# First x blocks in fp32 on two hardware queues with a cast on ScalarE, and the second group's transposes inside the first K bundle

## Chip, cores, metric

One core of one Trainium2 chip. The metric is the device time of one execution in microseconds (us), as the median of several runs. "Start" below is the first 30 us of the span, up to about the first V matmul; from some 36 us on the matmul engine (PE) has work without a break. SyncE is SP in the profile, ScalarE is ACT, VectorE is DVE, GpSimd is POOL.

## The reference, cut to what matters

```python
# x: (8, 4160, 192), weight: (8 heads, 7 taps)
w = exp(weight - max); w = w / (sum(w) + 1e-9)          # one row of 7 taps for each head
y[b, s, h, :] = sum_k w[h, k] * x[b, s + k - 6, h, :]   # causal convolution, 24 channels a head
y_prev = y shifted by one position
xk = mu_k * y + (1 - mu_k) * y_prev
xr = mu_r * y + (1 - mu_r) * y_prev
k = max(xk @ w_k, 0)                                    # 192 -> 1024
v = (k * k) @ w_v                                       # 1024 -> 192
out = sigmoid(xr @ w_r) * v
```

## The kernel before

x comes in blocks of 120 positions. A block is convolved on PE by a banded matrix for each head (`toe`, built from the softmax of the small `weight` row), copied out of PSUM, transposed on PE, evacuated, mixed with its predecessor (`diff`, `mix`), and multiplied by `w_k`. Blocks come in groups: the first four (3, 4, 4 and 5 blocks of a pair of batches) make up the start. PSUM is the memory that PE writes to, and an evacuation is a copy out of it. `xk` has 192 channels: K's upper half uses the first 128 of them, its lower half the other 64. A step is a stretch of positions that is mixed at once, and a K slot is the part of its K output that fills one PSUM buffer and is read by one relu. The start's loads and its order are the prologue:

```python
def prologue():
    nc.sync.dma_start(out=w_raw, in_=...)      # weight row, to all partitions
    nc.scalar.preload_act_table(AF.Exp)
    nc.vector.memset(ones_t, 1.0)
    x_tile(0, nc.vector)
    nc.vector.memset(zeros, 0.0)
    nc.gpsimd.affine_select(out=ident, ...)
    load_x(0)                                  # GpSimd; the DMA casts fp32 to bf16
    masks_band()
    warm(WARM)                                 # 16 matmuls that only keep PE's clock up
    ...
    softmax()                                  # Exp, then a tiny sigmoid that loads the other table
    make_toe()
    load_x(1); load_wk(); load_x(2); load_wr(); load_wv()     # all GpSimd, in this order
    ...                                        # mu_k, mu_r on SyncE
    for c in range(0, len(chunks(0)), 2):
        conv_mm(0, c)                          # 8 matmuls
    conv_out_first()                           # 5 copies, ScalarE and VectorE in turn
    warm(4)
    tr(0, 0)                                   # transposes, evacuations, diff, mix
    warm(2)
    ...conv(1, c)                              # second group
    warm(3)
    x_tile(3, nc.vector)
    load_x(3)

# main loop, one bundle of four K slots at a time
for part in (ns[:2], ns[2:]) if b == 0 else (ns,):
    k_section(part)                            # K matmuls: upper half, then lower half
    for n in part: k_relu(n)                   # ScalarE
    if part[:1] == ns[:1]: run(first, b)       # transposes of the next group, after K
```

`ring` is a pool of four PSUM buffers of two banks each; every convolution, transpose, K, V and R output takes its next buffer.

## Time and profile before

| | kernel before |
|---|---|
| time, median | 448.14 us (447.26 to 448.17, 3 runs; with a fourth of 447.44, taken beside the kernel after, 447.79) |
| profiled span | 445.9 us |
| PE busy | 433.8 us, 97% |
| first relu of K starts | 14.78 us |
| first V matmul starts | 29.95 us |
| last output is issued | 441.93 us |

How to read it: PE is full from about 36 us on, so the start decides. Two places in it serve as marks. The first relu shows how fast the chain "weight row, toe, convolution, copies, transposes, mix, K" is. The first V matmul shows when the hand-over to the dense part happens; a kernel whose first V matmul is earlier by some time issues its last output earlier by nearly the same: from the one to the other it takes 411.97 to 412.18 us in all 14 traces of this study.

Further lines of the order of time of the kernel before; the columns are start, duration, engine, line, operation, shapes, count, and in brackets the engine's idle time before and what ended it:

```profile
4.23 0.21 DVE L173 TENSOR_REDUCE w_max<-w_raw 128x8 f32<-128x56 f32 x1 [1.89 <-DMA w_raw<-in_weight_dram]
8.63 0.34 ACT L268 CAST y<-ps_c 120x216 bf16<-120x216 f32 x1 [2.14 <-PE ps_c L250]
19.01 2.98 PE L416 MATMUL ps_k<-xk,wk 128*128 128x512 bf16 x16 [1.13 <-DVE xk L397]
29.95 2.80 PE L505 MATMUL ps_v<-wv,k 128*128 128x192 bf16 x32 [0.60 <-ACT k_sb L457]
441.93 0.49 SPq L559 DMA_DIRECT2D out_dram<-o_tail  x1
```

The first copy out of PSUM is at 8.63; PE waits 1.13 us for the second step's xk before 19.01.

### The profile page before, as it was taken

What the parts mean: (1) busy time and instruction counts of PE and PEld (TensorE: products, weight loads), DVE (VectorE), ACT (ScalarE), POOL (GpSimd) and SP (SyncE); (2) the same over time, 40 slices, a digit from 0 to 9 for tenths busy, and PEclk for the clock granted to TensorE, in tenths of its full rate; (3) what the DMA queues carried; (4) which work ended last, traced back from release to release, by engine and by line L of the source; (5) the groups of instructions that cost most, each with busy time, mean ns of one, the idle gap of its engine ahead of it and who ended that gap; (6) DMA issues with size and microseconds to landing.
All of it is one profiled execution on the core that took longest, in us unless ns stands there. A gap on an engine that the chain in (4) does not pass through costs nothing.

```text
span 445.9 us, 9765 instructions
## 1 busy us (share of the span) xinstructions
PE 433.8 (97%) x3937; PEld 304.5 (68%) x3937; DVE 387.8 (87%) x702; ACT 353.7 (79%) x465; POOL 48.2 (11%) x70
## 2 busy tenths in 40 slices
PE   7889999999999999999999999999999999999995
PEld 3555766776866776676676677667667677766685
DVE  4899799889988989889978998889988898999972
ACT  3878888888897788888888788888988778777771
POOL 8650001102020100012020000010200000000000
PEclk9999999999999999999999999999999999999999
DMA  8998759979497693295798493485964562522113
GB/s 89 150 186 157 187 146 160 162 188 197 122 206 194 128 197 103 80 202 138 154 209 167 121 216 114 111 118 160 197 160 115 162 153 80 111 72 71 64 47 114
DMA packets 133184, 63.64 MB, mean 143 GB/s; under 512 B 84723, under 2 KB 132883, under 8 KB 133139
## 3 DMA queue, kind: packets, MB, share of 16 engines
q1 hardware_dynamic: 94834, 48.28, 41.1%
q0 software_dynamic: 38224, 14.68, 29.1%
q8 instruction: 31, 0.51, 0.5%
q14 instruction: 15, 0.11, 0.1%
q10 hardware_dynamic: 80, 0.05, 0.0%
HBM read 29.39 MB, written 36.99 MB: 149 GB/s over the span
## 4 chain that ended last, share of the span: by engine, by line
PE 87%; DVE 3%; DMA 3%; ACT 3%; POOL 2%; issue 1%; DVEq 0%
PE ps_k L416 37%; PE ps_v L505 37%; PE ps_r L500 4%; PE ps_r L501 4%; PE ps_c L250 4%; DMA xb<-in_x_dram 1%; DMA wk<-in_moe_w_k_dram 1%; ACT y L286 1%; DVE k L476 1%; POOL xb L122 1%; ACT r_sb L522 1%; DVE o_sb L532 1%; PE ps_vt L505 0%; DVE xk L397 0%; ACT k_sb L457 0%
## 5 line engine op out<-in xcount | busy, mean ns | idle before, releaser
L457 ACT ACTIVATE k_sb<-ps_k 128x1024 bf16<-128x1024 f32 x260 | 245.9, 1035 | 13.0 <-PE ps_k L416 9.8
L416 PE MATMUL ps_k<-xk,wk 64*128 64x512 bf16 (+3 forms) x1056 | 191.6, 373 | 2.5 <-DVE xk L397 1.7
L505 PEld LDWEIGHTS <-k 128*128 128x128 bf16 x2048 | 170.9, 98 | 14.9 <-issue 0.7
L505 PE MATMUL ps_v<-wv,k 128*128 128x192 bf16 x2048 | 179.4, 246 | 0.6 <-ACT k_sb L457 0.6
L476 DVE TENSOR_TENSOR k<-k_sb 128x1024 bf16<-128x1024 bf16 x256 | 168.2, 686 | 10.2 <-ACT k_sb L457 9.1
L416 PEld LDWEIGHTS <-wk 64*128 64x128 bf16 (+1 forms) x1056 | 66.4, 96 | 102.0 <-issue 56.0
L532 DVE TENSOR_TENSOR o_sb<-ps_v,r_sb 128x768 f32<-128x768 f32 x64 | 61.2, 957 | 26.6 <-PE ps_v L505 26.2
L522 ACT ACTIVATE r_sb<-ps_r 128x768 bf16<-128x768 f32 x64 | 53.1, 829 | 24.8 <-PE ps_r L501 24.8
L286 ACT CAST y<-ps_c 120x480 bf16<-120x480 f32 (+6 forms) x84 | 38.4, 515 | 32.8 <-PE ps_c L250 32.8
L122 POOL DMA_DIRECT2D xb<-in_x_dram x36 | 32.2, 898 | 168.9 <-PE ps_k L416 95.2
L500 PE MATMUL ps_r<-wr,xr 128*128 128x192 bf16 x256 | 47.4, 246 | 0.2 <-DVE o_sb L532 0.2
L501 PE MATMUL ps_r<-wr,xr 128*128 128x192 bf16 x256 | 47.4, 246 | 0.0
L397 DVE TENSOR_TENSOR xk<-xk,yT 128x1024 bf16<-128x1024 bf16 (+1 forms) x66 | 36.2, 549 | 2.3
L397 DVE TENSOR_TENSOR xr<-xr,yT 128x1024 bf16<-128x1024 bf16 (+1 forms) x66 | 36.2, 549 | 2.3
L250 PE MATMUL ps_c<-xb,toe 128*128 128x480 bf16 (+4 forms) x144 | 30.9, 321 | 1.9 <-DMA xb<-in_x_dram 1.9
L355 DVE TENSOR_TENSOR d<-yT 128x1536 bf16<-128x1536 bf16 (+4 forms) x38 | 31.8, 837 | 0.1
L394 DVE TENSOR_SCALAR xk<-d,mu 128x1024 bf16<-128x1024 bf16 (+1 forms) x66 | 27.5, 416 | 1.2
L501 PEld LDWEIGHTS <-xr 128*128 128x128 bf16 x256 | 25.0, 98 | 3.9 <-issue 0.5
L500 PEld LDWEIGHTS <-xr 128*128 128x128 bf16 x256 | 25.0, 98 | 3.5
L394 DVE TENSOR_SCALAR xr<-d,mu 128x1024 bf16<-128x1024 bf16 (+1 forms) x66 | 27.2, 412 | 0.0
L289 ACT CAST y<-ps_c 120x480 bf16<-120x480 f32 (+6 forms) x45 | 20.3, 501 | 8.0 <-PE ps_c L250 8.0
L250 PEld LDWEIGHTS <-toe 128*128 128x128 bf16 x144 | 12.8, 98 | 3.6 <-issue 1.3
(57 smaller groups left out, 79.3 us busy)
## 6 DMA issues: line engine op xcount, KB each, us to landing
out_dram<-o_sb SPq DMA_DIRECT2D x62, 384.0 KB, 3.1
y_dram<-y SPq DMA_DIRECT2D x10, 900.0 KB, 7.0
xb<-in_x_dram POOLq DMA_DIRECT2D x14, 480.0 KB, 8.7
xb<-in_x_dram POOLq DMA_DIRECT2D x6, 432.0 KB, 7.8
xb<-in_x_dram POOLq DMA_DIRECT2D x10, 192.0 KB, 6.4
y_dram<-y SPq DMA_DIRECT2D x3, 450.0 KB, 4.1
y_dram<-y SPq DMA_DIRECT2D x1, 810.0 KB, 5.7
xb<-in_x_dram POOLq DMA_DIRECT2D x2, 384.0 KB, 7.1
```

The lines of the kernel that those rows point to most:

```text
L250: nc.tensor.matmul(out=ps[:, :, :, i * G : (i + 1) * G], lhsT=toe[:, h, :], rhs=xbs[g][:, :nb, :, h * G : (h + 1) * G], start=True, stop=True,
L286: copy(out=yh[:, :, :, c0 : c0 + n], in_=ps[:BLK, :, :, 0:n])
L394: nc.vector.tensor_scalar(out=o, in0=d[:, sl, :L], scalar1=mu[:, i, part : part + 1], scalar2=None, op0=ALU.mult)
L397: nc.vector.tensor_tensor(out=o, in0=o, in1=yT[:, sl, c0 : c0 + L], op=ALU.add)
L416: nc.tensor.matmul(out=ps[:, i, f * L : (f + 1) * L], lhsT=wk[r, 0 if hi else 1, fs], rhs=xk[r, i if hi else 2, :L], start=start and f == ...
L457: nc.scalar.activation(out=k_sb, in_=ps.rearrange("p a b -> p (a b)"), func=AF.Relu)
L476: nc.vector.tensor_tensor(out=o, in0=i, in1=i, op=ALU.mult)
L500: nc.tensor.matmul(out=o, lhsT=hi, rhs=wr[:, 0, :], start=True, stop=False)
L501: nc.tensor.matmul(out=o, lhsT=lo, rhs=wlo, start=False, stop=True)
L505: nc.tensor.matmul(out=o, lhsT=k2s[s][:, f, t * P : (t + 1) * P], rhs=wv[:, f, :], start=(f == 0), stop=(f == NF - 1),)
L522: nc.scalar.activation(out=r_sbs[s, j], in_=ps, func=AF.Sigmoid)
L532: nc.vector.tensor_tensor(out=o_sb.rearrange("p (b t) d -> p b (t d)", b=2), in0=v_ps.pop((s, j)), in1=r_sbs.pop((s, j)), op=ALU.mult,)
```

## The change

Its intent: x for the first group no longer goes through GpSimd's queue, behind masks and three other issues, but comes in fp32 on the queues of SyncE and ScalarE at once, and ScalarE casts it. GpSimd starts on the second group's x and on `w_k` earlier. The small groups' convolution gets a bank layout with three copies in place of five. The second group's transposes move ahead of the first bundle's lower half of K, so that DVE has the second step's xk earlier. The diff's core:

```diff
+    def load_x_first(s, eng):
+        nb = groups[0][2]
+        for q0, q1, n0, n1 in ((0, P, 1, nb), (16, P, 0, 1), (HALO, 16, 0, 1)):
+            eng.dma_start(out=x_f32[q0:q1, n0:n1, s, :], in_=...)
...
         nc.scalar.activation(out=w_exp, in_=w_exp, func=AF.Exp)
+        xbs[0] = three.tile([P, GB, 2, D], BF16, tag="xb", name="xb")
+        for s in range(2):
+            nc.scalar.copy(out=xbs[0][:, : groups[0][2], s, :], in_=x_f32[:, :, s, :])
         nc.scalar.activation(out=w_sig, in_=w_exp[:, 0, 0:1], func=AF.Sigmoid)
...
+    def conv_small(g, copies):            # groups 0 to 2
+        tiles = [ring.tile([P, 2, BANK], FP32, tag="k", name="ps_c") for _ in range(2)]
+        banks = [t[:, i, 0 : nb * P] for t, i in ((tiles[0], 0), (tiles[1], 0), (tiles[0], 1))]
+        ...                               # 15 matmuls, bank by bank
+        for i, o in enumerate(banks):
+            copies[i](out=ys[g][i]..., in_=o[:BLK, :])
...
+        if ns[0] == 0:                    # k_section of the first half bundle
+            k_ps[0] = ring.tile([P, 2, BANK], FP32, tag="k", name="ps_k")
+            warm(k_ps[0], 3)
+            for n in ns:
+                k_mm(n, True, True)
+            run(first, 0)                 # the second group's transposes
+            for n in ns:
+                k_mm(n, False, False)
+            return
...
         nc.sync.dma_start(out=w_raw, in_=...)
+        nc.vector.memset(ones_t, 1.0)
+        nc.vector.memset(x_f32[0:32, 0, :, :], 0.0)
+        load_x_first(0, nc.sync)
+        load_x_first(1, nc.scalar)
         nc.scalar.preload_act_table(AF.Exp)
...
+        load_x(1, (0,))
         nc.gpsimd.affine_select(out=ident, ...)
-        load_x(0)
+        load_x(1, (1,))
+        load_wk(0, NF // 2)
         masks_band()
...
-        load_x(1)
-        load_wk()
+        load_wk(NF // 2, NF)
         load_x(2)
...
-        ...conv_mm(0, c); conv_out_first(); warm(4); tr(0, 0); warm(2); ...conv(1, c); warm(3)
+        conv(0, 0)
+        tr_first()
+        conv(1, 0)
```

Cut: `tr_first` (one evacuation on DVE, one on ScalarE), the fused mix of the first step, and renamings.

More of the change, by code (lines that the diff above doesn't have):

```diff
@@ L106, in x_tile, with load_x @@
             eng.memset(xb[:, nb - 1, :, :], 0.0)
-    def load_x(g):
+    def load_x(g, batches=(0, 1)):
         p, blk0, nb, _, _ = groups[g]
         xb = xbs[g]
-        for s in range(2):
+        for s in batches:
             b = 2 * p + s
@@ L129, in load_x @@
             )
+    def load_x_first(s, eng):
+        nb = groups[0][2]
+        for q0, q1, n0, n1 in ((0, P, 1, nb), (16, P, 0, 1), (HALO, 16, 0, 1)):
+            eng.dma_start(
+                out=x_f32[q0:q1, n0:n1, s, :],
+                in_=bass.AP(
+                    tensor=x.tensor,
+                    offset=x.offset + (s * S + n0 * BLK - HALO + q0) * D,
+                    ap=[[D, q1 - q0], [BLK * D, n1 - n0], [1, D]],
+                ),
+            )
+    x_f32 = three.tile([P, NF * STEP], FP32, tag="k2", name="x_f32")[:, 0 : groups[0][2] * 2 * D].rearrange(
+        "p (n s d) -> p n s d", s=2, d=D
+    )
     w_raw = const.tile([P, H, K], FP32)
@@ L155, with load_wk @@
     tails = [const.tile([P, 2, 2, P], BF16, tag=f"tail{i}", name=f"tail{i}") for i in range(2)]
-    def load_wk():
-        nc.gpsimd.dma_start(out=wk[:, 0, :], in_=moe_w_k[0:P, :])
-        nc.gpsimd.dma_start(out=wk[0:LO, 1, :], in_=moe_w_k[P:D, :])
-        nc.gpsimd.dma_start(out=wk[LO:P, 1, :], in_=moe_w_k[P:D, :])
+    def load_wk(f0, f1):
+        fs = slice(f0 * P, f1 * P)
+        nc.gpsimd.dma_start(out=wk[:, 0, fs], in_=moe_w_k[0:P, fs])
+        nc.gpsimd.dma_start(out=wk[0:LO, 1, fs], in_=moe_w_k[P:D, fs])
+        nc.gpsimd.dma_start(out=wk[LO:P, 1, fs], in_=moe_w_k[P:D, fs])
     def load_wr():
@@ L241, in conv_mm @@
         nb = groups[g][2]
-        if c == 0 and g > 0:
+        if c == 0:
             ys[g] = two.tile([P, GB, 2 * D], BF16, tag="y", name="y")
@@ L256, in conv_mm @@
                 )
-    def conv_out_first():
-        nb = groups[0][2]
-        ys[0] = [const.tile([P, nb, P], BF16, tag=f"y0{i}", name="y0") for i in range(3)]
-        for c, hs in enumerate(chunks(0)):
-            ps = conv_ps.pop((0, c))
-            c0, c1 = hs[0] * G, hs[-1] * G + G
-            n = min(c1, P) - c0
-            if n > 0:
-                for i, copy in enumerate((nc.scalar.copy, nc.vector.tensor_copy)):
-                    copy(out=ys[0][i][:BLK, :, c0 : c0 + n], in_=ps[:BLK, :, i, 0:n])
-            if c1 > P:
-                n = c1 - max(c0, P)
-                lo = ys[0][2][:BLK, :, :].rearrange("p n (s c) -> p n s c", s=2)
-                nc.scalar.copy(out=lo[:, :, :, c1 - P - n : c1 - P], in_=ps[:BLK, :, :, c1 - c0 - n : c1 - c0])
+    def conv_small(g, copies):
+        nb = groups[g][2]
+        ys[g] = [two.tile([P, 4, P], BF16, tag=f"y_small{i}", name="y_small") for i in range(3)]
+        tiles = [ring.tile([P, 2, BANK], FP32, tag="k", name="ps_c") for _ in range(2)]
+        banks = [t[:, i, 0 : nb * P] for t, i in ((tiles[0], 0), (tiles[1], 0), (tiles[0], 1))]
+        for i, o in enumerate(banks):
+            o = o.rearrange("p (n s c) -> p n s c", n=nb, s=2 if i == 2 else 1)
+            c0, c1 = (P, D) if i == 2 else (0, P)
+            for h in range(c0 // G, -(-c1 // G)):
+                a, b = max(c0, h * G), min(c1, h * G + G)
+                nc.tensor.matmul(
+                    out=o[:, :, :, a - c0 : b - c0],
+                    lhsT=toe[:, h, :],
+                    rhs=xbs[g][:, :nb, slice(0, 2) if i == 2 else slice(i, i + 1), a:b],
+                    start=True,
+                    stop=True,
+                )
+        for i, o in enumerate(banks):
+            copies[i](out=ys[g][i][:BLK, :nb, :].rearrange("p n c -> p (n c)"), in_=o[:BLK, :])
     def conv_out(g, c, copy, copy_lo=None):
@@ L316, in tr @@
         p, blk0, nb, _, _ = groups[g]
-        if blk0 == 0 and j == 0:
-            new_yT(p)
         ps = ring.tile([P, 2, 2 * BANK], BF16, tag="k", name="ps_t")
@@ L325, in tr, with tr_first @@
                     out=view[:, (i - 4 * j) // 2, c, i % 2, :],
-                    in_=ys[g][c][:BLK, i, :] if g == 0 else ys[g][:BLK, i, c * P : (c + 1) * P],
+                    in_=ys[g][c][:BLK, i, :] if g < 3 else ys[g][:BLK, i, c * P : (c + 1) * P],
                     identity=ident[:BLK, :BLK],
                 )
-        def evacuate(cs):
-            for i in todo[::2]:
-                n = min(2, nb - i)
-                c0 = YC + (blk0 + i) * BLK
-                nc.vector.tensor_copy(
-                    out=yTs[p][:, cs, c0 : c0 + n * BLK].rearrange("p c (n t) -> p c n t", n=n),
-                    in_=view[:, (i - 4 * j) // 2, cs, :n, :],
-                )
-        if g > 0:
-            evacuate(slice(0, 3))
-        else:
-            for part, cs in enumerate((slice(0, 2), slice(2, 3))):
-                evacuate(cs)
-                diff(0, cs)
-                mix(0, 0, part)
+        for i in todo[::2]:
+            n = min(2, nb - i)
+            c0 = YC + (blk0 + i) * BLK
+            nc.vector.tensor_copy(
+                out=yTs[p][:, :, c0 : c0 + n * BLK].rearrange("p c (n t) -> p c n t", n=n),
+                in_=view[:, (i - 4 * j) // 2, :, :n, :],
+            )
+    def tr_first():
+        nb = groups[0][2]
+        n = nb * BLK
+        new_yT(0)
+        tiles = [ring.tile([P, 2, 2 * BANK], BF16, tag="k", name="ps_t") for _ in range(2)]
+        for c in range(3):
+            for i in range(nb):
+                c0 = c % 2 * n + i * BLK
+                nc.tensor.transpose(
+                    out=tiles[c // 2][:, 0, c0 : c0 + BLK], in_=ys[0][c][:BLK, i, :], identity=ident[:BLK, :BLK]
+                )
+        yT = yTs[0]
+        nc.vector.tensor_copy(
+            out=yT[:, 0:2, YC : YC + n], in_=tiles[0][:, 0, 0 : 2 * n].rearrange("p (c t) -> p c t", c=2)
+        )
+        nc.scalar.copy(out=yT[:, 2, YC : YC + n], in_=tiles[1][:, 0, 0:n])
+        for part, cs in enumerate((slice(0, 2), slice(2, 3))):
+            diff(0, cs)
+            mix(0, 0, part)
     diffs, xks, xrs = {}, {}, {}
@@ L393, in mix @@
             o = t[:, sl, :L]
+            if s == 0 and i == 0:
+                return go(o, sl, 0, P)
             nc.vector.tensor_scalar(
@@ L406, in k_mm @@
         xk = xks[s]
-        if start:
+        if start and n not in k_ps:
             k_ps[n] = ring.tile([P, 2, BANK], FP32, tag="k", name="ps_k")
@@ L428, in k_section @@
             return k_mm_tail(ns[0], steps[s][0])
-        h = len(ns) // 2 if ns[0] > 0 else len(ns)
+        if ns[0] == 0:
[7 more added lines that the diff above has]
+            return
+        h = len(ns) // 2 if ns[0] > 2 else len(ns)
         for n in ns[:h]:
@@ L569, in conv @@
     def conv(g, c):
+        if g < 3:
+            act_, dve_ = nc.scalar.copy, nc.vector.tensor_copy
+            return conv_small(g, (act_, dve_ if g == 0 else act_, act_))
         conv_mm(g, c)
@@ L574 @@
     for g, (p, blk0, nb, fb, on_pe) in enumerate(groups):
-        nx = -(-len(chunks(g)) // 2)
+        nx = 1 if g < 3 else -(-len(chunks(g)) // 2)
         if g == 0:
@@ L580 @@
         elif p == 0:
-            xs = {2: [0, 0], 3: [1, 1], 4: [2, 2, 3, 3], 5: [4, 4, 5, 5]}[g]
+            xs = {2: [0], 3: [1, 1], 4: [2, 2, 3, 3], 5: [4, 4, 5, 5]}[g]
         else:
@@ L625, in run, with warm @@
             fn(*a)
-    def warm(n):
-        ps = ring.tile([P, 2, BANK], FP32, tag="k", name="warm")
+    def warm(ps, n):
         for i in range(n):
@@ L636, in prologue @@
         )
+        nc.vector.memset(ones_t, 1.0)
+        nc.vector.memset(x_f32[0:32, 0, :, :], 0.0)
+        load_x_first(0, nc.sync)
+        load_x_first(1, nc.scalar)
         nc.scalar.preload_act_table(AF.Exp)
-        nc.vector.memset(ones_t, 1.0)
-        x_tile(0, nc.vector)
         nc.vector.memset(zeros, 0.0)
+        x_tile(1, nc.vector)
+        load_x(1, (0,))
         nc.gpsimd.affine_select(
@@ L649, in prologue @@
         )
-        load_x(0)
+        load_x(1, (1,))
+        load_wk(0, NF // 2)
         masks_band()
-        warm(WARM)
-        x_tile(1, nc.vector)
+        warm(ring.tile([P, 2, BANK], FP32, tag="k", name="warm"), WARM)
         x_tile(2, nc.vector)
+        nc.vector.memset(wr[:, 2:4, :], 0.0)
         masks_mod8()
-        nc.vector.memset(wr[:, 2:4, :], 0.0)
         softmax()
         make_toe()
-        load_x(1)
-        load_wk()
+        load_wk(NF // 2, NF)
         load_x(2)
@@ L670, in prologue @@
             nc.gpsimd.memset(t, 0.0)
-        for c in range(0, len(chunks(0)), 2):
-            conv_mm(0, c)
-        conv_out_first()
-        warm(4)
-        tr(0, 0)
-        warm(2)
-        for c in range(0, len(chunks(1)), 2):
-            conv(1, c)
-        warm(3)
+        conv(0, 0)
+        tr_first()
+        conv(1, 0)
         x_tile(3, nc.vector)
@@ L695 @@
                     k_relu(n)
-                if part[:1] == ns[:1]:
+                if b > 0:
                     run(first, b)
```

## The prediction

> **What bounds the kernel now.** I read the busy shares first, then the stretches of the span, then the chain of waits and the order of instructions for the first 40 us, because the change touches only the start.
>
> ```profile
> PE 433.8 (97%) x3937; PEld 304.5 (68%) x3937; DVE 387.8 (87%) x702; ACT 353.7 (79%) x465; POOL 48.2 (11%) x70
> ...
> 0.00:8.00 8.00, 5.78 (x16) 2.07 (x16) 4.51 (x15) 3.02 (x4) 6.83 (x17) 1.00 0.59 54
> 8.00:13.00 5.00, 4.26 (x34) 2.38 (x34) 2.56 (x9) 2.33 (x8) 3.18 (x6) 1.00 1.28 176
> 13.00:19.00 6.00, 4.56 (x52) 3.37 (x52) 4.35 (x11) 4.76 (x8) 5.72 (x9) 1.00 1.31 147
> 19.00:24.00 5.00, 3.79 (x30) 1.85 (x31) 4.90 (x13) 4.72 (x8) 0.97 (x2) 1.00 1.36 155
> 24.00:36.00 12.00, 10.90 (x99) 7.36 (x99) 11.41 (x23) 9.24 (x16) 6.05 (x8) 1.00 1.55 183
> 36.00:48.00 12.00, 11.87 (x108) 8.30 (x105) 10.83 (x19) 10.18 (x15) 0.00 (x0) 1.00 0.74 169
> ```
>
> The columns after the length are PE, weight loads, DVE, ACT and POOL. From 36 us on PE is full (11.87 of 12.00), and stays so until 440 us. Nothing after 36 us changes, so the change is worth exactly the time by which PE reaches its dense part earlier, and no more. Before 36 us PE is not full, and DVE and ACT are: from 19 to 24 us DVE has 4.90 and ACT 4.72 of 5.00. PE's 5.78 us in the first 8 us are 16 warming matmuls, no work of the kernel.
>
> Who sets the start is in the chain that ended last and in the order of time:
>
> ```profile
> 4.98 1.43 POOL xb L122 x2
> 6.41 6.39 DMA wk<-in_moe_w_k_dram
> ...
> 17.03 6.65 DMA xb<-in_x_dram
> ...
> 8.06 0.66 PE L250 MATMUL ps_c<-xb,toe 128*128 128x144 bf16 x8 [0.70 <-DMA xb<-in_x_dram]
> ...
> 13.14 1.03 PE L416 MATMUL ps_k<-xk,wk 128*128 128x256 bf16 x8 [0.35 <-DVE xk L397]
> 14.35 0.61 PE L416 MATMUL ps_k<-xk,wk 64*128 64x256 bf16 x8 [0.17 <-DVE xk L397]
> 14.78 3.77 ACT L457 ACTIVATE k_sb<-ps_k 128x1024 bf16<-128x1024 f32 x4 [1.24 <-PE ps_k L416]
> ...
> 20.41 3.77 ACT L457 ACTIVATE k_sb<-ps_k 128x1024 bf16<-128x1024 f32 x4 [0.28 <-PE ps_k L416]
> 24.43 1.35 ACT L286 CAST y<-ps_c 120x480 bf16<-120x480 f32 x3 [0.24 <-PE ps_c L250]
> ```
>
> The first convolution starts at 8.06 us. The wait is put down to the x block, but the weights for it (toe) were ready only at 7.14 + 0.76 = 7.90 us: the two are tied. First K matmul 13.14, its wk landed at 6.41 + 6.39 = 12.80: again tied with xk. From the first relu at 14.78 us ScalarE has work until about 31 us with idle of 0.28 and 0.24 only. So three nearly equal chains run beside each other: ScalarE's relus, DVE's mixes, and GpSimd's loads, whose block for the fourth group lands at 17.03 + 6.65 = 23.68.
>
> **What the Trainium skill says.** "ScalarE: Activation LUTs", section "What ACT_TABLE_LOAD costs": 1283 ns a table load, 186 ns + 0.833 ns per element an ACTIVATE with immediates. This trace agrees: both loads take 1.28, and a 1024-wide relu has a mean of 1035 against 1039. By it a 576-wide cast is an estimated 0.67 us. "DMA: Bandwidth & Descriptors", section "Latency and other measured facts": first byte after 0.6 us from a hardware queue, 1 us from GpSimd's. The trace shows less of a difference to landing: 3.4 us for the weight row on SyncE's queue, 3.8 for an x block of 96 KB on GpSimd's. "TensorE: Matmul & The Clock Gate", Part 1: half rate until some 3.4 us of activity, and half rate again after idle. The granted clock here reads 1.00 throughout, yet the first warming matmuls are spaced by 0.43 us and those after 6.1 us by 0.2, as the page says.
>
> **The change part by part.**
> (1) *First x blocks on two hardware queues.* Four GpSimd issues disappear (0.72 + 0.75 + 0.57 + 0.71 = 2.75 us of that queue, from 1.58 on); six come on SyncE and ScalarE, 0.4 to 0.6 each, from 0.8 us. The second on each waits for a memset that ends near 1.5, the third is out near 2.6; with the 3 to 3.4 us to landing of that queue, x is there at 5.6 to 6.0. Exp comes at 4.73 as before; two casts of 0.67 then run 5.8 to 7.1, the second table load to 8.4, the small sigmoid to 8.6. The convolution now waits for toe alone. Toe hangs on the weight row, which now shares the queues with x: 7.9 to 8.3. So the first convolution starts at about 8.1, as before: **gain 0**. ScalarE is free just as its first copy is due (8.6).
> (2) *Convolution, copies, transposes of the first group.* 15 small matmuls in place of 8, at the 62 ns of eight in 0.50 us: 0.93. Five ScalarE/DVE copies that alternated bank by bank (8.63 to 10.66) become three, each on a bank of its own: ScalarE 8.6 to 9.1 (a 384-wide one has mean 502 ns), DVE 9.0 to 9.55 (382 ns for 216, 333 for 168, so about 0.56), ScalarE to 9.75. Transposes of the first two parts end near 9.8 (before near 10.4, evacuation at 11.09). One DVE evacuation of 720 (517 ns) to 10.35, difference 0.43 to 10.8. The fused mix: the trace has this operation at 278 ns for 64 and 349 for 128, 1.1 ns an element, so 0.75 to 0.78 for 512 (before 0.35 + 0.43 and a gap), to 11.6. xk is there at 11.6 instead of 13.0, its lower part at 12.4 instead of 14.3: **1.4 and 1.9 us earlier**.
> (3) *K bundle.* PE does the second convolution at 10.1 to 11.1, three warming matmuls to 11.75, K's upper half 1.03 to 12.8. wk's first half is issued at 2.5 to 4.3 instead of 6.41 to 8.04; with its old 6.5 us it lands by 10.8. Then come the second group's 12 transposes, 0.65, which stood after K's lower half before, and only then the lower half, 0.45. First relu at 14.0 to 14.3, against 14.78. So most of the 1.4 us is **spent again here**, on 0.65 of transposes and on warming; net 0.5 to 0.8.
> (4) *What the moved transposes buy.* DVE evacuates the second group from about 13.5 instead of 15.74, so the second step's xk is ready near 16.7 instead of 18.9, and PE's idle of 1.13 us before 19.01 shrinks. But then the ring of four PSUM buffers holds PE: the second step's second slot needs the fourth relu's buffer, 14.2 + 3.8 = 18.0.
> (5) *ScalarE from there.* Relus 14.2 to 18.0; third group's copies, three of 512 (0.6 each) in place of five (1.90), to 19.7; second relus 19.7 to 23.4 instead of 20.41 to 24.18; fourth group's copies at 23.5 instead of 24.43.
> (6) *Loads.* GpSimd issues 2.75 us less and 1.7 us more (six pieces of wk for three). Nearly all bytes that stood before the fourth group's block remain, but start about 1.7 us earlier. I expect it at about 22, before the 23 us at which PE asks for it.
> Sum: 0.6 from the first relu, 0.15 from copies, 0.3 to 0.5 from the two short idles of ScalarE that an earlier load and xk remove: **about 1.2 us** at the hand-over to PE near 30 us. Nothing after it differs.
>
> **Rivals.**
> (a) *ScalarE's cast is late.* If x lands at 7 because three queues share 16 DMA engines, casts end at 8.4, the table load behind them at 9.7, the first copy starts 1.1 us late and the gain is gone: 447.8 to 448.3. For it: the old load of x had the engines nearly to itself; against it: about 1 MB in the first 6 us is less than what the queues move later (180 GB/s as written in bf16).
> (b) *The relu is no bound, DVE and the loads are.* Then the 1.9 us of parts 2 and 4 come through: 446.0 to 445.5. For it: DVE is busy 4.90 of 5.00 and is what PE waits for at 19.01. Against it: ScalarE has only 0.5 us of idle in 16.
> (c) *PE cools.* Six warming matmuls between convolution and transposes go. If the clock halves, K's 1.03 us becomes 2 and the others follow: 447.5 to 449. Against it: gaps on PE stay under 0.7 us.
> (d) *The loads stay the bound*, landing no earlier than 23.7: gain 0.2.
>
> **Range and chances.** Before: 447.26 to 448.17, median 448.14, mean 447.87. Minus 1.2, leaning a little to (b): 446.6. One part of noise (0.5) and one of the rivals give 445.3 to 448.0. A change of 2% would be 9 us; all idle of PE in the span is 445.9 - 433.8 = 12 us, much of it at the very start and end, so neither side of 2% can be expected.
>
> **What would show it.** Right: first convolution at 7.9 to 8.4 on toe, not x; the casts done by 7.3; first K near 11.7; first relu near 14.2; relus of the second step near 19.7; nothing changed per instruction after 36 us. Wrong: a convolution or first copy that waits for the cast or table load; a first relu before 13.5 (more gain) or after 14.8 (none); PE's first long wait on the fourth group's load; K matmuls in the first bundle spaced at twice the old 0.13 us.

## The result, and the profile after

Ratios are the mean time of one kernel's fast runs over that of the other's fast runs of the same rounds, so not quite the ratio of the medians that are quoted.

| | before | after |
|---|---|---|
| time, median, first comparison | 447.79 us (447.26 to 448.17) | 448.14 us (447.48, 447.63, 448.65, 448.74) |
| ratio, 95% interval | | 1.0008 (0.9986 to 1.0031) |
| profiled span | 445.9 | 445.8 |
| weight row landed | 4.23 | 5.38 |
| first convolution | 8.06 | 8.70 |
| ScalarE's first copy out of PSUM | 8.63 | 10.26 |
| first relu | 14.78 | 15.16 |
| first V matmul | 29.95 | 29.49 |
| last output issued | 441.93 | 441.53 |

No gain, instead of 1.2 us: 448.14 lies 0.14 us above the range. The four runs fall into two pairs: 447.48 and 447.63 at a mean granted clock of 1.000, 448.65 and 448.74 at 0.994. Both things need an explanation: the 1 us that is missing in the good runs, and the other 1.1 us in the others.

The order of time of the kernel after:

```profile
5.38 0.21 DVE L191 TENSOR_REDUCE w_max<-w_raw 128x8 f32<-128x56 f32 x1 [2.09 <-DMA w_raw<-in_weight_dram]
7.59 1.24 ACT L198 CAST xb<-x_f 128x576 bf16<-128x576 f32 x2 [1.47 <-DMA x_f<-in_x_dram]
8.28 0.76 DVE L245 TENSOR_TENSOR toe<-w_per,band 128x384 bf16<-128x384 bf16 x2
8.70 1.02 PE L291 MATMUL ps_c<-xb,toe 128*128 128x72 bf16 x15 [1.52 <-DVE toe L245]
8.85 1.28 ACT L200 ACT_TABLE_LOAD   x1
10.26 0.84 ACT L299 CAST y_small<-ps_c 120x384 bf16<-120x384 f32 x2
13.13 1.03 PE L455 MATMUL ps_k<-xk,wk 128*128 128x256 bf16 x8 [0.30 <-DVE xk L412]
15.16 3.77 ACT L506 ACTIVATE k_sb<-ps_k 128x1024 bf16<-128x1024 f32 x4 [1.38 <-PE ps_k L455]
29.49 2.80 PE L554 MATMUL ps_v<-wv,k 128*128 128x192 bf16 x32 [0.60 <-ACT k_sb L506]
441.53 0.49 SPq L608 DMA_DIRECT2D out_dram<-o_tail  x1
```

Two chains are late here. The row landed at 5.38 instead of 4.23, and with it toe (8.28 against 7.14) and the first convolution, which waits for toe: toe is written by two instructions, of 0.36 and 0.48 us, and the convolution starts after the first, which ends at 8.64. And the last piece of x landed at 7.49, not at 5.6 to 6.0, so ScalarE casts from 7.59 until 8.83, loads the other table until 10.13, runs the tiny sigmoid until 10.35, and only then copies (its record begins at 10.26, overlapping the sigmoid's end), although the convolution had ended at 9.72; DVE's copy of its own bank began at 9.57. The chain that ended last passes through these three before it comes to the copy; columns start, duration, what:

```profile
2.24 5.25 DMA x_f<-in_x_dram
8.17 0.67 ACT xb L198
8.85 1.28 ACT L200
```

The view of the transfers in the first 8 us, with size and the median us from issue to landing, kernel before and then after:

```profile
w_raw<-in_weight_dram SPq DMA_DIRECT2D x1, 28.0 KB, 3.4
```

```profile
x_f<-in_x_dram ACTq DMA_DIRECT2D x1, 192.0 KB, 5.1
x_f<-in_x_dram SPq DMA_DIRECT2D x1, 192.0 KB, 5.2
w_raw<-in_weight_dram SPq DMA_DIRECT2D x1, 28.0 KB, 4.6
```

The row takes 4.6 us instead of 3.4, with the same issue at the same time. The Trainium skill, "DMA: Bandwidth & Descriptors", section "Issuing engines are not separate DMA queues", says that transfers started by different engines run on the same 16 DMA engines and interleave, and that starting them on several saves only issue time. The longer landing agrees with interleaving: in the packed traces each of the row's 128 packets takes 14 ns in both kernels, but the last of them starts at 3.85 us before and at 5.00 after. No run here separates the DMA engines from the rest of the path.

### The profile page after: what moved, and what is told of

The parts are those of the page before. It is cut to its first block, busy times and chain, and to the rows that moved or that the text cites. A ratio compares the mean times of both kernels' runs of the same rounds, so it can differ in the third digit from the quotient of the medians.

```text
span 445.8 us, 9727 instructions
## 1 busy us (share of the span) xinstructions
PE 429.0 (96%) x3889; PEld 304.2 (68%) x3952; DVE 387.7 (87%) x696; ACT 354.5 (80%) x462; POOL 47.1 (11%) x69
## 3 DMA queue, kind: packets, MB, share of 16 engines
q0 software_dynamic: 37696, 14.39, 27.9%
## 4 chain that ended last, share of the span: by engine, by line
PE 87%; DVE 5%; ACT 4%; issue 2%; DMA 1%; DVEq 0%; SPq 0%; ACTq 0%
PE ps_v L554 37%; PE ps_k L455 36%; PE ps_r L549 4%; PE ps_r L550 4%; PE ps_c L271 4%; DVE k L525 2%; ACT y L313 2%; DMA x_f<-in_x_dram 1%; ACT k_sb L506 1%; DVE o_sb L581 1%; DVE d L392 1%; ACT r_sb L571 0%; PE ps_vt L554 0%; ACT y L316 0%; DVE xk L436 0%
## 5 line engine op out<-in xcount | busy, mean ns | idle before, releaser
L455 PE MATMUL ps_k<-xk,wk 64*128 64x512 bf16 (+3 forms) x994 | 188.1, 373 | 5.8 <-ACT y L313 0.6
L313 ACT CAST y<-ps_c 120x480 bf16<-120x480 f32 (+4 forms) x78 | 36.2, 523 | 31.4 <-PE ps_c L271 31.4
L122 POOL DMA_DIRECT2D xb<-in_x_dram x34 | 30.8, 914 | 171.5 <-PE ps_k L455 95.1
L271 PE MATMUL ps_c<-xb,toe 128*128 128x480 bf16 (+2 forms) x120 | 28.8, 338 | 0.2
L316 ACT CAST y<-ps_c 120x480 bf16<-120x480 f32 (+4 forms) x41 | 19.0, 514 | 8.0 <-PE ps_c L271 8.0
L271 PEld LDWEIGHTS <-toe 128*128 128x128 bf16 x120 | 10.9, 98 | 1.3 <-issue 0.5
```

Source lines behind the costliest of these rows:

```text
L271: nc.tensor.matmul(out=ps[:, :, :, i * G : (i + 1) * G], lhsT=toe[:, h, :], rhs=xbs[g][:, :nb, :, h * G : (h + 1) * G], start=True, stop=True,
L313: copy(out=yh[:, :, :, c0 : c0 + n], in_=ps[:BLK, :, :, 0:n])
L455: nc.tensor.matmul(out=ps[:, i, f * L : (f + 1) * L], lhsT=wk[r, 0 if hi else 1, fs], rhs=xk[r, i if hi else 2, :L], start=start and f == ...
```

## The experiments

Theory at the outset: two ends late, the row by shared DMA engines and the first copy by ScalarE's order, make up the missing microsecond. Rivals: one of the two alone; the moved transposes as the cost; the loads behind; PE's clock. Runs e1 to e4 were on one chip, e5 to e8 on another, e9 to e11 on a third, e12 on a fourth; each has runs of the kernel before on the same chip. All twelve gave right results.

| run | time, median (range) us | ratio to before, 95% | row landed | first relu | first V | last output issued | span |
|---|---|---|---|---|---|---|---|
| e1 sigmoid before casts | 446.93 (446.90 to 447.11) | 0.9989 (0.9977 to 1.0002) | 5.37 | 14.67 | 29.00 | 440.98 | 445.2 |
| e2 x by GpSimd | 447.63 (447.02 to 448.46) | 1.0008 (0.9995 to 1.0022) | 4.15 | 13.53 | 29.29 | 441.33 | 445.3 |
| e3 both x on SyncE | 449.44 (448.40 to 449.83) | 1.0039 (1.0026 to 1.0052) | 4.83 | 15.54 | 29.87 | 442.05 | 446.6 |
| e4 only part 1 | 449.75 (449.44 to 450.11) | 1.0052 (1.0040 to 1.0065) | 4.97 | 16.73 | 31.78 | 443.75 | 448.0 |
| e5 after, again | 447.53 (447.44 to 447.57) | 1.0001 (0.9988 to 1.0014) | 5.36 | 15.12 | 29.45 | 441.52 | 445.8 |
| e6 more warming | 447.73 (447.72 to 448.54) | 1.0009 (0.9997 to 1.0022) | 5.37 | 15.46 | 29.80 | 441.78 | 446.0 |
| e7 transposes behind | 448.03 (447.98 to 448.79) | 1.0019 (1.0006 to 1.0033) | 5.40 | 14.57 | 30.09 | 442.08 | 446.3 |
| e8 e2, loads reordered | 445.64 (445.60 to 446.48) | 0.9964 (0.9952 to 0.9977) | 4.23 | 13.86 | 28.19 | 440.24 | 444.2 |
| e9 before, loads reordered | 447.35 (447.25 to 447.94) | 0.9995 (0.9981 to 1.0008) | 4.17 | 15.10 | 30.19 | 442.17 | 446.2 |
| e10 e8, mask later | 445.73 (445.45 to 446.16) | 0.9960 (0.9948 to 0.9972) | 4.20 | 13.99 | 28.32 | 440.38 | 444.4 |
| e11 no warming in K | 448.46 (447.61 to 449.31) | 1.0020 (1.0006 to 1.0033) | 5.41 | 16.08 | 30.41 | 442.49 | 446.7 |
| e12 e1, three buffers | 446.77 (446.65 to 446.89) | 0.9979 (0.9965 to 0.9992) | 5.34 | 14.39 | 28.72 | 440.70 | 444.9 |

The columns from "row landed" on are of the profiled run. The medians of before were 447.37 (e1 to e4), 447.36 (e5 to e8), 447.62 (e9 to e11) and 447.80 (e12).

### e1: the sigmoid, and so the table load, before the casts

```diff
         nc.scalar.activation(out=w_exp, in_=w_exp, func=AF.Exp)
+        nc.scalar.activation(out=w_sig, in_=w_exp[:, 0, 0:1], func=AF.Sigmoid)
         xbs[0] = three.tile([P, GB, 2, D], BF16, tag="xb", name="xb")
         for s in range(2):
             nc.scalar.copy(...)
-        nc.scalar.activation(out=w_sig, in_=w_exp[:, 0, 0:1], func=AF.Sigmoid)
```

> The changed kernel with the small sigmoid, and so its table load, ahead of the two casts. Theory T (the new x path is what ate the gain, by two things: a weight row that lands 1.15 us later, and casts that push the 1.28 us table load in front of the first copy): table load 6.1 to 7.4, casts still 7.6 to 8.85 because x lands then, first copy near 9.35 instead of 10.35, first relu near 14.2 instead of 15.16, end 0.6 to 1.0 us earlier than the changed kernel, about 446.9. Rival R1 (the late weight row alone is the cause): first copy waits for something else, end unchanged. Rival R2 (ScalarE is not what carries the first 30 us any more): first relu earlier by 1 us but the end by under 0.3.

The order of time:

```profile
6.13 1.28 ACT L196 ACT_TABLE_LOAD   x1
7.67 1.24 ACT L199 CAST xb<-x_f 128x576 bf16<-128x576 f32 x2
8.69 1.02 PE L290 MATMUL ps_c<-xb,toe 128*128 128x72 bf16 x15 [1.64 <-DVE toe L244]
9.74 0.86 ACT L298 CAST y_small<-ps_c 120x384 bf16<-120x384 f32 x2 [0.83 <-PE ps_c L290]
```

The table load now fills the wait for x. ScalarE's first copy comes at 9.74 instead of 10.26, the first relu at 14.67 instead of 15.16, the first V matmul at 29.00 instead of 29.49: the 0.49 us goes through whole. That is half of what was expected (9.35 for the copy, 14.2 for the relu). What remains of the lateness is the convolution at 8.69. The copy waits for PE's last matmul (8.69 + 1.02 = 9.71), not for its own bank's six; e12 takes that up.

### e2: first x block by GpSimd, all else of the change kept

```diff
-        nc.vector.memset(x_f32[0:32, 0, :, :], 0.0)
-        load_x_first(0, nc.sync)
-        load_x_first(1, nc.scalar)
+        x_tile(0, nc.vector)
...
-        load_x(1, (1,))
-        load_wk(0, NF // 2)
+        load_x(0)
         masks_band()
+        load_x(1)
+        load_wk(0, NF // 2)
```

(the casts and the first half of `load_x(1)` go too)

> The changed kernel with the first x blocks loaded by GpSimd as before (cast by the DMA, no ScalarE cast), all other parts of the change kept. Theory T: weight row lands at 4.2 again, toe 7.9, first convolution at 8.1, first copy 8.6, first relu 14.0 to 14.3 as the prediction had it, and the end 0.8 to 1.2 us earlier than the changed kernel unless the loads of the fourth group, 1 to 2 us later again, hold it. Rival R2 (the moved transposes and smaller convolutions cost, not x): first relu at 14.8 or later, end like the changed kernel. Rival R3 (the loads are the bound): PE waits for the fourth group's x near 23.7 and the end is as before the change.

The order of time:

```profile
7.55 1.02 PE L285 MATMUL ps_c<-xb,toe 128*128 128x72 bf16 x15 [0.66 <-DVE toe L239]
23.15 0.98 PE L265 MATMUL ps_c<-xb,toe 128*128 128x240 bf16 x8 [2.31 <-DMA xb<-in_x_dram]
```

The row is back at 4.15, the convolution at 7.55, and the first relu at 13.53 (14.0 to 14.3 expected): 1.63 us earlier than in the kernel after. 0.49 of these are the table load (e1); the other 1.14 are row and x. But the time does not follow. PE waits 2.31 us for the fourth group's x, which is behind `w_r` and `w_v` in GpSimd's queue, so the first V matmul is at 29.29. The start was made faster than its loads: rival (d) of the prediction, waiting behind rival (a).

### e3: both x blocks on SyncE's queue

```diff
-        load_x_first(1, nc.scalar)
+        load_x_first(1, nc.sync)
```

> The changed kernel with both x blocks on SyncE's queue behind the weight row, none on ScalarE's. Theory T, in the form that ScalarE's x block takes turns with the weight row: the row lands at 4.3 to 4.5 instead of 5.38 and toe is ready near 7.6; x lands at 7.5 to 8.5, so the casts, not toe, set the first convolution at 9 to 9.5, and the end is within 0.5 of the changed kernel. If the row still lands at 5.2 or later, it is GpSimd's x block or its own queue that delays it, and that form of T falls.

The row lands at 4.83 (4.3 to 4.5 expected), between 4.23 and 5.38: with less going on beside it, it is less late. The first x block lands earlier than in the kernel after (its cast starts at 6.58 us) but the second later (8.54), so nine of the convolution's matmuls wait until 9.26; the first relu is at 15.54, and the time is worse. Three of its five runs have a clock of 0.993 and take 449.44 to 449.83, the other two 448.40 and 448.44; this is taken up under e11.

### e4: part 1 alone, on the kernel before

```diff
+        nc.vector.memset(x_f32[0:32, 0, :, :], 0.0)
+        load_x_first(0, nc.sync)
+        load_x_first(1, nc.scalar)
         nc.scalar.preload_act_table(AF.Exp)
-        x_tile(0, nc.vector)
...
-        load_x(0)
```

(with the casts as in the change)

> The kernel before with part 1 alone: first x blocks in fp32 on two hardware queues and cast by ScalarE; everything else as before. Theory T: the row lands near 5.3, toe near 9.0, casts to 8.9, table load behind them to 10.3, first copy near 10.3 instead of 8.63, first relu 16.0 to 16.4 instead of 14.78, end 0.8 to 1.5 us later than before. Rival R2: first relu within 0.3 of 14.78, end as before.

Part 1 alone costs 2.4 us (449.75 against 447.37), more than the 0.8 to 1.5 expected, but not all of it is x. ScalarE's first copy is 0.78 us later than in the kernel before (9.41 against 8.63), and DVE's first multiply of the mix starts 0.75 later (12.93 against 12.18). Then this multiply takes 1.42 us where it took 0.35, while GpSimd's memset of `tail`, which stood at 15.23 before, runs beside it:

```profile
12.93 1.42 DVE L415 TENSOR_SCALAR xk<-d,mu 128x512 bf16<-128x512 bf16 x1
13.20 1.01 POOL L692 MEMSET tail<- 128x512 bf16 x2
```

Of the 1.83 us by which the first V matmul is late, 1.07 belong to this one instruction. In the kernel after the fused mix stands in its place and takes 0.75 us, as foreseen, so this part of the loss does not carry over, and the change can't be read as e4's loss plus gains of the same size. In e2 a multiply beside the same memset takes 1.23 us instead of 0.49; no run isolates the two. The row lands at 4.97 here. The row's landing orders itself by what else is being loaded: 4.15 to 4.23 with x on GpSimd only, 4.83 without ScalarE's queue, 4.97 with both hardware queues but GpSimd's next x block issued later (1.98 instead of 1.31 us), 5.38 with all three.

### e5: the kernel after, once more, on the chip of e6 to e8

No edit.

> The changed kernel, unaltered. In its first four runs two were at 447.5 with granted clock 1.000 and two at 448.7 with 0.994, so its median hides two kinds of run. Theory C (rival (c) of the prediction in part: in some runs the TensorE clock falls back for one stretch of about 3.4 us among the gaps of 7 to 13 us, which costs about 1.1 us): again a split into two groups about 1.1 us apart, the later one with the lower clock; the upper group lies above the kernel before. Rival (plain scatter between chips): one group, spread under 0.5 us.

447.53, all five runs between 447.44 and 447.57, clocks 0.997 to 1.000. At full clock the kernel after is even with the kernel before, within 0.2 us either way.

### e6: more warming matmuls

```diff
-    WARM = 16
+    WARM = 23
...
+        for _ in range(4 if g == 0 else 0):
+            nc.tensor.matmul(out=tiles[1][:, 1, :], lhsT=ones_t, rhs=zeros, start=True, stop=True)
```

> The changed kernel with 23 warming matmuls at the start instead of 16 and 4 after the first convolution, in PE's idle time and in a PSUM bank that nothing else uses; the order of the rest is unchanged. Theory C: all runs in the fast group, 447.2 to 447.6, none near 448.7. Rival: the same spread as the unaltered changed kernel; or later by 0.2 to 0.8, if the added matmuls stand in the way of the transposes.

No run below 0.997, but the unaltered kernel (e5) had none either, so this says nothing on the cure. Its own price shows: first relu 15.46, time 0.2 us longer. One of its runs took 448.54 at a clock of 0.998, and one of the kernel before 448.72 at 1.000 (with e9 to e11): late runs without a loss of clock occur too, and are unexplained.

### e7: the second group's transposes behind K again

```diff
                 k_mm(n, True, True)
-            run(first, 0)
             for n in ns:
...
-                if b > 0:
+                if part[:1] == ns[:1]:
                     run(first, b)
```

> The changed kernel with the second group's transposes behind the first K bundle again, where the kernel before has them. By the prediction's part 3 the first relu comes 0.6 to 0.8 us earlier (near 14.4 instead of 15.16) and the second step's xk 0.6 us later (near 17.7 to 18.2, PE idle before it again). If ScalarE carries the start, the end is 0.3 to 0.7 us earlier; if DVE and the transposes carry it, 0.3 to 0.7 us later. The change's title says its author expected the second.

The order of time:

```profile
14.57 1.94 ACT L505 ACTIVATE k_sb<-ps_k 128x1024 bf16<-128x1024 f32 x2 [0.75 <-PE ps_k L455]
19.28 2.98 PE L455 MATMUL ps_k<-xk,wk 128*128 128x512 bf16 x16 [1.58 <-DVE xk L436]
```

The first relu is 0.55 us earlier than in e5 (14.57 against 15.12), as the prediction's part 3 has it. Yet the first V matmul is 0.64 us later (30.09), and the time 0.5: PE waits 1.58 us for the second step's xk. (Some 0.24 of this may not be the order: DVE's multiply for that xk takes 0.97 us here and 0.73 in e5.) The moved transposes are a gain, and the first relu is not by itself what sets the hand-over.

### e8: e2, and the fourth group's x ahead of w_r and w_v

```diff
         load_x(2)
-        load_wr()
-        load_wv()
...
         x_tile(3, nc.vector)
         load_x(3)
+        load_wr()
+        load_wv()
```

(on top of e2)

> The kernel with the first x blocks loaded by GpSimd as before (run e2, whose first relu came at 13.53 but whose PE then waited 2.31 us for the fourth group's x until 23.15), with that block's load put ahead of those of w_r and w_v. If the loads are what ate e2's gain: x for the fourth group lands before 21.5, the fourth group's convolution starts without a wait on a load, the third step's relus near 25.0 instead of 26.32, and the end is 1.0 to 1.5 us earlier than e2 in runs of full clock, 445.5 to 446. If w_r or w_v now come late, PE waits on them at 23 to 30 us instead and the gain is under 0.3.

The order of time:

```profile
21.21 1.27 PE L265 MATMUL ps_c<-xb,toe 128*128 128x240 bf16 x8
28.19 2.80 PE L548 MATMUL ps_v<-wv,k 128*128 128x192 bf16 x32 [0.60 <-ACT k_sb L500]
```

The convolution that waited 2.31 us for its x in e2 has no wait at 21.21. The first V matmul is 1.76 us earlier than before, the last output 1.69, the span 1.7, the median 1.72: what PE gains at the hand-over arrives at the end. With e10, from which it isn't told apart, this is the fastest kernel, and faster than the kernels before and after.

### e9: the same order of loads in the kernel before

The edit is that of e8, on the kernel before.

> The kernel before with nothing but the order of e8: the fourth group's x is loaded ahead of w_r and w_v. It tells how much of e8's gain (445.64 against 447.36) is the order alone. In the kernel before the fourth group's convolution waited 1.20 us for that load, but ScalarE behind it idled only 0.24. If ScalarE carries the start: 0.2 to 0.5 us earlier than before, and the rest of e8's 1.7 is the change's parts 2 to 4 with the first x blocks left on GpSimd. If the load alone was the bound: 1.0 us or more.

447.35 against 447.62, ratio 0.9995 with an interval over 1: the 0.3 us that the order of loads alone may bring is not told from noise. So e8's gain is that of the change's parts 2 to 4, which the loads had hidden; it takes both. The profiled run is the slowest of the five (447.94; `w_k` landed late in it), so its marks in the table are not typical.

### e10: the mask after the second group's x

```diff
         load_x(0)
-        masks_band()
         load_x(1)
+        masks_band()
```

(on top of e8)

> Kernel e8 with the two mask instructions of GpSimd behind the second group's x loads instead of ahead of them, so that these are issued 0.6 us earlier (4.3 instead of 4.9). In e8 the second half of the second group's convolution waited 0.62 us for that x, and the first relu came at 13.86 instead of 13.53 in e2. Expected: that wait gone, first relu 13.5 to 13.7, end 0.2 to 0.4 us earlier than e8. If the DMA engines and not the issue set the landing: no change. If the masks now hold toe (needed at 7.1): later.

No difference from e8 (0.9960 and 0.9964). The second group's x was issued earlier, but now the first block landed later, and the convolution's second half waited for it at 8.49. Here an issue that came sooner took its time from another transfer.

### e11: no warming matmuls in the K section

```diff
             k_ps[0] = ring.tile([P, 2, BANK], FP32, tag="k", name="ps_k")
-            warm(k_ps[0], 3)
```

> The changed kernel without the three warming matmuls ahead of the first K bundle. They end before xk is ready (12.8 against 13.1), so they hold nothing back. If the clock falls back in some runs for want of PE work (rival (c)), more runs than the changed kernel's two of nine fall in a group about 1 us later with a granted clock of 0.994 or less. If the clock has nothing to do with it: 447.4 to 447.6 in all five, as the changed kernel had on its second chip.

Three of five runs have a clock of 0.994 or 0.995 and take 448.46 to 449.31; the two at 1.000 take 447.61 and 447.87. The profiled run is one of the three. Two stretches of its span; columns: length, busy us (and count) of PE, weight loads, DVE, ACT and POOL, granted clock, DMA share, GB/s:

```profile
8.00:11.41 3.41, 1.41 (x24) 1.05 (x25) 1.55 (x5) 3.18 (x6) 2.84 (x5) 1.00 1.28 176
11.41:14.82 3.41, 2.99 (x26) 2.19 (x25) 2.40 (x5) 2.02 (x4) 3.41 (x7) 0.50 1.27 139
```

In e11 the clock is half from 11.41 to 14.82, exactly one window of 3.41 us. The K matmuls of the first bundle, which take 1.03 us in the kernel after, take 1.74:

```profile
13.34 1.74 PE L455 MATMUL ps_k<-xk,wk 128*128 128x256 bf16 x8 [0.42 <-DVE xk L412]
```

The Trainium skill, "TensorE: Matmul & The Clock Gate", Part 1, gives a window of 3413 ns that runs freely, and half rate after an idle one; the length agrees. The window before it was not idle, though: PE was busy for 1.41 of 3.41 us. The three matmuls left out in e11 stand at 12.02 in the kernel after, behind that window, so their absence did not make it, and three such runs of five against two of nine may be chance: e11 is where the slow window was seen, not a test of what causes it.

The windows lie elsewhere in other runs: the warming matmuls pass from 0.43 us apart to about 0.2 at 4.7 us in e11's trace, at 5.5 in the kernel after's and at 6.1 in the kernel before's. So the kernels are compared by the emptiest stretch of 3.41 us that their traces have after 6 us, wherever it begins. PE is busy for 0.89 us of it in the kernel after (7.18 to 10.59), 0.89 in e7 and e11, 1.04 in e3 and 1.10 in e2 (19.74 to 23.15, the wait for x); these five have runs at a clock of 0.993 to 0.996 that are mostly 0.5 to 1.7 us late (2 of 9, 2 of 5, 3 of 5, 3 of 5, 2 of 5). In the kernel before (2.21), e6 (2.61), e8 (1.83), e9 (2.28) and e10 (1.56) no run is below 0.997; nor in e1 (1.07), e4 and e12 (1.47 each), which with five runs each may be luck. (A mean of 0.997 needs no explanation: in e5's trace the clock is half only after 442.9 us, where PE has ended.) The order was found after the fact. Only e11's slow window was seen in a trace; that the slow runs of e3, e7 and the kernel after have such a window too is inferred from their clock and size.

### e12: e1, with a PSUM buffer of its own for each bank

```diff
-        tiles = [ring.tile(...) for _ in range(2)]
-        banks = [t[:, i, 0 : nb * P] for t, i in ((tiles[0], 0), (tiles[1], 0), (tiles[0], 1))]
+        tiles = [ring.tile(...) for _ in range(3 if g == 0 else 2)]
+        banks = [t[:, i, 0 : nb * P] for t, i in
+                 ((tiles[0], 0), (tiles[1], 0), (tiles[2], 0) if g == 0 else (tiles[0], 1))]
```

> The kernel of e1 (sigmoid before the casts) with one edit: the three banks of the first group's convolution lie in three PSUM buffers instead of two, so that the first and the third bank no longer share one. Theory (the copy waits for the last matmul into its buffer, not for its own bank's six): ScalarE's first copy starts at 9.15 to 9.3 us instead of 9.74, while DVE's, whose bank had a buffer of its own before, stays at 9.56; the first evacuation of transposes starts near 10.4 instead of 10.80, the first K matmul near 12.25 instead of 12.64, the first relu at 14.2 to 14.4 instead of 14.67, the first V matmul 28.6 to 28.8 instead of 29.00, and the time 446.4 to 446.8, ratio to the kernel before 0.998. Rival 1 (ScalarE is held by something else, for example the cast or its issue): first copy still at 9.7, first relu 14.67, time 446.9. Rival 2 (the copy comes earlier but DVE's copy at 9.56 or the third group of transposes sets the evacuation): first copy at 9.2, first relu gains less than 0.2.

The order of time:

```profile
8.66 1.02 PE L290 MATMUL ps_c<-xb,toe 128*128 128x72 bf16 x15 [1.62 <-DVE toe L244]
9.35 0.86 ACT L298 CAST y_small<-ps_c 120x384 bf16<-120x384 f32 x2 [0.42 <-PE ps_c L290]
```

ScalarE's copy starts 0.69 us after the convolution's start, before its last matmul has ended, instead of 1.05. So the wait was for the buffer. (9.15 to 9.3 had been expected; it starts at 9.35.) First relu and first V matmul come 0.28 us earlier than in e1. The expected 14.2 to 14.4 holds. The time, 446.77 at a ratio of 0.9979, is within the noise of e1's; that the 0.28 us reaches the end is seen in the last output (440.70 against 440.98) and the span, not in the medians.

## Why the prediction was wrong

The frame held: instructions after the start are unchanged, and what the first V matmul gains is found again at the last output (0.46 and 0.40 us in the kernel after, 1.76 and 1.69 in e8). The sum of 1.2 us did not:

| term | predicted | measured | shown by |
|---|---|---|---|
| first relu | 14.2, 0.6 earlier | 15.16, 0.4 later | trace |
| first relu to first V matmul | 0.45 to 0.65 shorter | 0.84 shorter | trace |
| first V matmul | 1.2 earlier | 0.46 earlier | trace |
| after the last output's issue | nothing | 0.25 longer | 14 traces |
| clock | full | 0.997 to 1.000 in 7 runs of 9; 0.994 and some 1.1 us late in two | runs; mechanism from e11 |

**Step (1) failed: "x is there at 5.6 to 6.0".** It took the 3 to 3.4 us of a row that was alone on its queue for loads that share the DMA engines. They took 5.1 to 5.7, the last piece of x landed at 7.49, and the row was 1.15 us late itself; where the prediction gave "7.9 to 8.3" for toe's readiness, its first part was ready at 8.64 and its second at 9.04. The casts were right (0.67 each), but 1.8 us late, and the table load behind them came to stand before the first copy. This is rival (a), which the text named, with "casts end at 8.4" and "the gain is gone: 447.8 to 448.3", and weighed too little: it compared bytes with the rate of the dense part, not the landing of small loads issued together. e1 shows 0.49 us for the table load, e2 another 1.14 for x and the row.

A reading of the kernel before was also off, without harm to the sum: toe and x were called tied, with toe ready at 7.90. The convolution needs only toe's first instruction, which ended at 7.50, and it waited for x, whose last piece landed at 7.93; in e9, with toe at the same 7.14 but x landed by 7.20, it starts at 7.55. One trace of the same start can thus differ from another by 0.5 us there.

**Step (2) failed in part.** Each of the three copies was taken to wait for its own bank, "ScalarE 8.6 to 9.1". It waited for the last of 15 matmuls, 1.02 us after the first (0.93 predicted), because the first bank shared a buffer with the third. In the kernel after, the table load hid this; with it out of the way (e1) it costs 0.28 us at the first relu, by e12.

**Step (3) held, and its reading failed.** The moved transposes do delay the first relu by about 0.6 us (e7: 0.55). But they are no loss: without them the hand-over is 0.64 us later.

**Steps (4) and (5) were mis-sized.** The first relu to the first V matmul shrinks by 0.84, more than forecast, though the second step's xk is ready only at 18.28 (16.7 predicted, 18.95 before) and its relus start at 20.22 (19.7 predicted, 20.41 before). That xk, not ScalarE alone, sets the stretch (e7), and rival (b) was half right: three chains run beside each other, and a gain in one shows only when the others are early too.

**Step (6) held.** It put the fourth group's x at about 22, and the part that the convolution needs lands at 22.40 (23.68 before), just ahead of the convolution at 22.54. It leaves no room, though: with a first relu at 14.39 (e12) PE waits 0.36 us for it, and in e2, where GpSimd has the first block's issues back and the load lands at 23.02, it waits 2.31.

**Rival (c), the clock, was put aside on "gaps on PE stay under 0.7 us".** They were 1.52 before the convolution and 1.06 before the transposes. A lost window is the likely reason for the two runs of the first four at 448.7, by their clock and size, and so for the median at 448.14; no trace of them was kept. The other runs are at 447.5, 0.9 us from the predicted time.

**A term that no part had.** From the issue of the last output to the end of the span it takes 3.98 to 3.99 us in the five traces without x on the hardware queues (before, e2, e8, e9, e10), and 4.24 to 4.27 in the eight with x on both (after, e1, e4, e5, e6, e7, e11, e12), with the spans to 0.01 us from the packed traces. So 0.40 us at the last output became 0.15 in the span.

What stays open: why the end takes 0.25 us longer with loads on both hardware queues (and 0.57 in e3, with SyncE's alone); why a multiply on DVE takes up to four times as long in e4; how much of the row's delay is due to each of the other loads, of which only the order by dose was seen; and whether the slow runs of e3, e7 and the kernel after have the slow window that e11's trace shows.

## What to carry to other kernels

At a kernel's start a load is not free because its queue is: issue first what the longest chain needs, and take the landing time of loads issued together, not of one alone, for the next step. Before a part is judged by the mark it moves, look for the next mark after it, and check that the loads behind can keep up: here the same parts 2 to 4 were worth nothing measurable with the loads in the old order (e2) and 1.7 us with two of them swapped (e8). A matmul engine that is busy less than half the time in one window may run the next at half clock, as in e11 (1.41 of 3.41 us), and where the windows lie differs from run to run, so look at every run's clock before reading a median.

## What the Trainium skill lacked or had wrong

- "DMA: Bandwidth & Descriptors", sections on latency and on issuing engines: they give a first-byte time and say that queues interleave on the same engines, but no figure for how much later a small load lands when others are issued with it. Here a 28 KB row took 3.4 us to land with x on GpSimd's queue and 4.6 with x on two hardware queues; 192 KB of x took 5.1 to 5.2. Spreading did not merely save nothing: the row landed at 4.83 with x on one hardware queue (e3) and at 5.38 with x on two.
- "TensorE: Matmul & The Clock Gate", Part 1: it gives the window's length, which the runs confirm (3.41 us at half clock), but no busy share at which a window counts as idle. Here a window with PE busy for 1.41 of 3.41 us, and no gap above 1.96 us, was followed by half clock (e11); in e4's trace, where the clock came up at about 6.6, PE is busy for 1.54 of the 3.41 us from 13.40, two windows later, and the clock stays full.
- No page has it: from the last output's issue to the end of the span, 4.24 to 4.27 us in kernels that load x on SyncE's and ScalarE's queues at the start, 3.98 to 3.99 in those that do not.
